# Moving the row scaling and the folds within the first 66 slots of a fused top-k attention and expert kernel

## The chip, the cores and the metric

The kernel runs on one core of one Trainium2 chip. The metric is the device time of one execution, in microseconds (us); lower is better. The engines are TensorE (PE, with its weight loads PEld), VectorE (DVE), ScalarE (ACT), GpSimd (POOL) and the queue of SyncE (SP), which here only issues DMAs. Each engine works through its own list of instructions in order, and waits on semaphores for what others produce.

## The reference: what is computed

Attention in which each query keeps only its 32 largest scores, and then a layer of eight experts of which each token takes one:

```python
batch, n_heads, seq, head_dim = (8, 8, 576, 64)
scores = scale * np.matmul(q, k.transpose(0, 1, 3, 2))
kth = np.partition(scores, -top_k, axis=-1)[..., -top_k:-top_k + 1]
scores = np.where(scores >= kth, scores, -1000000000.0)
attn = np.exp(scores - np.max(scores, axis=-1, keepdims=True))
attn = attn / (np.sum(attn, axis=-1, keepdims=True) + 1e-09)
x = np.matmul(attn, v)             # then (B, H, S, D) -> (B*S, H*D) = (4608, 512)
logits = x @ w_gate                # 8 experts; the largest logit takes the token
h = np.maximum(x_sorted[lo:hi] @ w1[e], 0.0)     # 512 -> 1024
y_sorted[lo:hi] = h @ w2[e]                      # 1024 -> 512
out = gate_w[:, None] * y
```

## The kernel before

**Slots.** The attention is cut into tiles of 128 queries by 576 keys, and two tiles make one slot. The main loop (L1217) makes 144 passes, i = 0 to 143: 18 slots for each of the 8 batches. A batch has four units of two heads; two units share nine slots (four slots of the first, one of both units' last 64 queries, four of the second). Below, "slot 12" is the pass with i = 12.

**One slot on VectorE.** `fold` (L307) takes the maximum `h` (L313) and the minimum `l` (L314) of the two halves of the next slot's scores. `fold_on` (L317) folds `h` once more: its maximum goes to `few` (L320), its minimum to `hl`. That minimum is made either on DVE (L328) or, when `aside_too` holds, on POOL by two integer operations, sum (L325) and difference (L326). `lists` (L345, L349) takes the eight largest of `l` and of the halves of `hl`. `search` (L351) then finds the 32 largest in four rounds, r = 0 to 3: MAX8 (L372) on both tiles and, in all but the last, MATCH_REPLACE (L382), which takes the eight found away. With `soon`, `fold_on` for the next slot comes after round r = 1; without it, before the last round's MAX8. From r = 2 on, `tick` (L332) puts one small step from the list `aside` behind each instruction: divisors, choice of experts, ranks, and the table of blocks.

**The other engines in a slot.** In round 0, POOL makes the bias `nbias` (L378). After the search, ACT makes `low` (L393) and `w` (L409); POOL subtracts, `w = s - w` (L418, one instruction per tile), and stores `doubt` (L399); ACT copies the scores of a later slot out of PSUM (L304), copies the transposed weights of the slot before (L444 or L442, L461), and makes the exponentials (L426) of this slot's `w`. PE makes scores (L297), transposes (L437), output products (L474, L485), and pieces of the expert blocks (L948, L965). The order on PE, ACT and DVE is the order of the code; on POOL most instructions are kept in it by `in_turn` (L250), while its indirect DMAs (L590 scatters rows of x, L857 stores rows of the result) are placed by the scheduler.

**The end of a unit.** `ending` (L1080) is a generator that a slot with tile 3 starts. It yields names of places, and the loop calls `at_place(name)` (L1176) where it may go on: "relu" copies outputs out of PSUM (L476, L492) and makes divisors (L496 to L501), "rows" (L1109) scales on POOL: `logits` (L511, then L513 and L514, or L516 in a batch's first unit), and `rows` (L525, 128x640). In the kernel before, "relu" and "rows" both stand behind `less` and `doubts` (L1242, L1243), and "relu" ahead of the scores of L304. For the last unit of a batch the generator goes on to the choice, the ranks, the scatter and the table that says which expert blocks can be loaded.

**Crowded slots.** `k.crowded` is set by the scaling of rows (L520), by stores (L1036) and by scatters (L1072). The next slot then doesn't search with `soon`. The integer fold is used only where 0 < i < `QUIET` (48) and the slot isn't crowded.

Of the kernel before, what the change touches and what calls it, by code (L numbers as in the profile page):

```python
# [44 lines left out]
def kernel(  # L45
# [48 lines left out]
    B, U, P, _ = qk.shape  # L94
# [37 lines left out]
    k = SimpleNamespace()  # L132

    def open_pools(st, exact):
        for name, bufs in (
            ("load", 2), ("att", 2), ("xp", 1 if exact else 2), ("small", 2),
            ("wp", 1 if exact else 2), ("mlp", 2),
        ):
            setattr(k, name, st.enter_context(tc.tile_pool(name=name, bufs=bufs)))
        for name, bufs in (("ps_s", 2), ("ps_t", 2), ("ps_m", 2)):  # L140
            pool = tc.tile_pool(name=name, bufs=bufs, space=bass.MemoryType.PSUM)
            setattr(k, name, st.enter_context(pool))
        k.exact = exact
        k.apart = k.between = k.crowded = False

    def load_unit(b, u, parts=False):
        n = SimpleNamespace(b=b, u=u)
# [102 lines left out]
    def in_turn(put):  # L250

        if not k.exact:
            tc.keep_in_program_order(put)
        return put
# [62 lines left out]
    def fold_on(f, aside_too=False):  # L317

        f.few = k.att.tile([P, 2, LW], F32, name="few", bufs=3)
        nc.vector.tensor_tensor(f.few[:, :, 0:QF], f.h[:, :, 0:QF], f.h[:, :, QF:HF], op=ALU.max)  # L320
        hl = k.att.tile([P, 2, QF], I32, name="hl", bufs=1)
        f.hl, f.aside = hl[:, :, :].bitcast(F32), aside_too
        if aside_too:
            one, other, more = (a.bitcast(I32) for a in (f.h[:, :, 0:QF], f.h[:, :, QF:HF], f.few[:, :, 0:QF]))
            in_turn(nc.gpsimd.tensor_tensor(hl, one, other, op=ALU.add))  # L325
            in_turn(nc.gpsimd.tensor_tensor(hl, hl, more, op=ALU.subtract))  # L326
        else:
            nc.vector.tensor_tensor(f.hl, f.h[:, :, 0:QF], f.h[:, :, QF:HF], op=ALU.min)  # L328

    aside = []  # L330

    def tick():  # L332

        while aside:
            if next(aside[0], "end") != "end":
                return
            aside.pop(0)
# [10 lines left out]
            for j, away in enumerate((f.l[:, m, :], f.hl[:, m, 0:QF // 2], f.hl[:, m, QF // 2:QF])):  # L348
                nc.vector.max(out=f.few[:, m, QF + 8 * j:QF + 8 * j + 8], in_=away)  # L349

    def search(tiles, s, f, then=lambda: None, soon=False, behind=lambda: None):  # L351

        m_all = range(2)
        tops = k.small.tile([P, 2, TOP_K], F32, name="tops", bufs=4)
        if k.exact:
            src = [s[:, m, :, :].rearrange("p j k -> p (j k)") for m in m_all]
            width = S
        else:
            src = [f.few[:, m, 0:QF] for m in m_all]
            width = LW  # L360
            if not f.aside:
                lists(f)
        behind()
        scr = k.att.tile([P, 2, width], F32, name="scr", bufs=1)
        nbias = k.small.tile([P, 2], F32, name="nbias", bufs=3)
        R = TOP_K // 8

        for r in range(R):
            if r == R - 1 and not soon:
                then()  # L370
            for m in m_all:
                nc.vector.max(out=tops[:, m, r * 8:(r + 1) * 8], in_=src[m])  # L372
                if r > 1:
                    tick()
            if r == 1 and soon:
                then()
            if r == 0:
                in_turn(nc.gpsimd.tensor_scalar_mul(nbias, tops[:, :, 0], -scale))  # L378
            if r < R - 1:
                for m in m_all:  # L380
                    first = r == 0 and not k.exact
                    nc.vector.match_replace(  # L382
                        out=src[m] if first else scr[:, m, :], in_to_replace=tops[:, m, r * 8:(r + 1) * 8],
                        in_values=src[m], imm_value=NEG,
                    )
                    if r > 1:
                        tick()
                    src[m] = f.few[:, m, :] if first else scr[:, m, :]
                if first and f.aside:
                    lists(f)  # L390
        thr = tops[:, :, TOP_K - 1]
        low = k.small.tile([P, 2], F32, name="low", bufs=3)
        nc.scalar.activation(low, thr, AF.Copy, scale=STEEP)  # L393

        def doubts():
            n, i = tiles[0]
            at = n.b * U + n.u
            over = doubt[:, at:at + 2, 2 * NC, :] if tails(tiles) else doubt[:, at, 2 * i:2 * i + 2, :]
            k.last_pool = in_turn(nc.gpsimd.tensor_tensor(  # L399
                over, f.few[:, :, QF + 7:LW:8], _inner(thr, NL), op=ALU.subtract  # L400
            )).ins

        return low, nbias, doubts
# [581 lines left out]
    FIRST = 13  # L985
    ARRIVED = 13
    AHEAD = 3
    QUIET = 48
    ON_CHIP = 3
    KEEP = 3 * PIECES  # L990
    BETWEEN = 2
# [1 line left out]
    with fast:  # L993
# [86 lines left out]
        def ending(b, u):  # L1080
# [68 lines left out]
            if new:  # L1149
                if b == B - 1:  # L1150
                    slot_i = slot_last
                    steps = end_table(slot_i, slot_long, new, half, full)
                else:
                    slot_i = k.small.tile([1, 2, NSLOT], I32, name="slot_i")
                    steps = table(slot_i, new, False)
                aside.append(steps)
                yield "weights"
                yield "pool"
                yield "weights"
                yield "pool"  # L1160
                through(steps)
                coming.extend((slot_i[0:1, 0, j:j + 1], slot_i[0:1, 1, j:j + 1]) for j in range(new))
            if b == B - 1:
# [10 lines left out]
        late = []  # L1174
# [25 lines left out]
        def loop():  # L1200
# [16 lines left out]
            for i, (b, g) in enumerate(work):  # L1217
                tiles = tiles_of(i)
                u, tile = g[0]
                if tile == 0 and u % 2 == 0:  # L1220
                    open_unit(tiles[0][0])
                if tails(tiles):
                    open_unit(tiles[1][0])

                then, quiet = lambda: None, 0 < i < QUIET and not k.crowded
                behind = lambda: None
                if i + 1 < len(work):
                    def behind():
                        f_of[i + 1] = fold(s_of[i + 1])

                    then = lambda: fold_on(f_of[i + 1], quiet)
                    if i:
                        behind()
                        behind = lambda: None
                low, nbias, doubts = search(tiles, s_of[i], f_of.pop(i), then, quiet, behind)
                k.crowded = False
                at_place("small")
                w_of[i] = depths(s_of[i], low)
                less(s_of.pop(i), w_of[i])
                doubts()  # L1240
                at_place("pool")
                at_place("relu")  # L1242
                at_place("rows")  # L1243
                put_stores()
                scatter(1)
                at = i % per_batch
                if at == FIRST and b:
                    rate = level(b) * PIECES / (U * NT)
                credit += rate * len(g)
                room = left  # L1250
                if b == B - 1 and at >= ARRIVED:
                    room -= KEEP
                    credit = room / (len(work) - i)
                share = {0: 0.5, 1: 1.2, 2: 1.6, 3: 0.5, 2 * NC: 1.4}[tile]
                now = max(0, min(int(credit * share + 0.5), room))
                credit -= now
                clock = i
                if i + AHEAD < len(work):
                    s_of[i + AHEAD], steps = scores(got_of.pop(i + AHEAD))
                    for step in steps:  # L1260
                        step()
                evacuate()
                at_place("turn")
                turns = turning(i - 1) if i else iter(())
                next(turns, None)
                part = min(BETWEEN, now - now // 2)
                rest = pieces(part)
                next(turns, None)
                rest = pieces(now - now // 2 - part + rest)
                weights(tiles, w_of[i], nbias)  # L1270
                next(turns, None)
                evacuate()
                if i + AHEAD + 1 < len(work):
                    multiply(i + AHEAD + 1)
                if tile == NC - 1:
                    end = ending(b, u)
                    late.append([end, next(end)])
                at_place("products")
                at_place("weights")
                credit = min(credit + pieces(now // 2 + rest), 6 * rate)  # L1280
# [152 lines left out]
```

## Time and profile before

| what | value |
|---|---|
| median of 3 runs | 1304.83 us (1302.8 to 1308.25) |
| the profiled execution | 1303.64 us, its span 1302.0 us |
| granted TensorE clock, mean | 0.967 |
| L418 on POOL, w = s - w | x288, 407.0 us busy, 1434 ns each; idle before it 342.6, waiting for ACT's L409 |
| L372 on DVE, MAX8 on 168 elements | x576 from `scr`, 165.9 us, 316 ns each |
| L313 and L314 on DVE, 128x576 | x143 each, 108.9 and 109.3 us, 761 and 764 ns |
| L320 on DVE, 128x288 | x144, 79.2 us, 550 ns |
| L328 on DVE, 128x288 | x114, 52.3 us, 459 ns |
| L325 and L326 on POOL, the integer fold | x30 each, 793 and 834 ns |
| L525 on POOL, 128x640 | x32, 42.0 us, 1312 ns |
| L476 on ACT, outputs out of PSUM | x64, 25.1 us; idle before it 32.4, waiting for PE's L474 |

A line of the profile names the source line, the engine, the operation, what is written and read, shape and count; behind the bar stand busy time, mean duration of one, and the idle time just before. An instruction that an engine has begun but that can't go on counts as busy, so a duration above the usual one of its kind is also something to look for. The page's second part shows busy tenths in 40 slices of the span. In the timeline each row is start, duration, engine, line, operation; in square brackets is the idle time before it and what ended it. Rows of the same kind that follow each other are merged (x2).

### The profile page before, as it was taken

To read this page: it belongs to the slowest core of one execution; us is meant where nothing else is said; L and a number is where in the kernel's file an instruction comes from. 1 tells how busy PE (TensorE), PEld (TensorE's weight loads), DVE (VectorE), ACT (ScalarE), POOL (GpSimd) and SP (SyncE) were. 2 spreads that over 40 slices of the span, in tenths; PEclk is the share of its full clock that TensorE was granted. 3 is DMA by queue.
4 is the path that set the end of the run, shared out by engine and by line. 5 is a ranking of instruction groups with operands and counts; after the bars stand their busy time and mean duration, and the time that the engine had idled before them with its cause. 6 is when DMAs were issued, how large, how long until landed. Compare 5 with 4: busy or idle time off the path is not lost. (4 is left out here: it accounts for less than half of the span.)

```text
span 1302.0 us, 24603 instructions
## 1 busy us (share of the span) xinstructions
PE 1193.9 (92%) x7654; PEld 836.4 (64%) x7654; DVE 1065.2 (82%) x4589; ACT 931.6 (72%) x2136; POOL 716.9 (55%) x867
## 2 busy tenths in 40 slices
PE   6777776899989999999999999999999999999998
PEld 3444443665666556666666666666666677789975
DVE  8999999999999999999999999999999954000000
ACT  4888877898888888888788888798888861112121
POOL 4777776777755575658555755576557643000010
PEclk9888888899999999999999999999999999999999
DMA  5000112741374148533945465447555458986682
GB/s 151 30 30 30 30 38 94 277 166 38 123 267 160 39 139 306 183 111 122 331 135 213 142 240 179 171 137 250 175 176 188 162 206 261 354 311 230 213 291 87
DMA packets 98797, 220.95 MB, mean 170 GB/s; under 512 B 5341, under 2 KB 26333, under 8 KB 98656
## 3 DMA queue, kind: packets, MB, share of 16 engines
q1 hardware_dynamic: 91424, 199.00, 44.4%
q0 software_dynamic: 6416, 19.97, 4.2%
q8 instruction: 62, 1.02, 0.3%
q14 instruction: 79, 0.65, 0.2%
q10 hardware_dynamic: 816, 0.31, 0.1%
HBM read 195.88 MB, written 24.17 MB: 169 GB/s over the span
## 5 line engine op out<-in xcount | busy, mean ns | idle before, releaser
L418 POOL TENSOR_TENSOR w<-s,w 128x576 f32<-128x576 f32 x288 | 407.0, 1434 | 342.6 <-ACT w L409 342.5
L948 PE MATMUL ph<-xTs,w 128*128 128x128 f32 x2112 | 259.7, 277 | 4.5 <-ACT xTs L839 3.0
L948 PEld LDWEIGHTS ph<-xTs,w 128*128 128x128 f32 x2112 | 248.0, 192 | 23.0 <-issue 17.6
L965 PE MATMUL py<-w,hT 128*128 128x512 f32 x528 | 248.2, 599 | 3.3 <-ACT hT L953 3.2
L426 ACT ACTIVATE w<-w,nbias 128x576 f32<-128x576 f32 x288 | 224.1, 793 | 2.8 <-POOL w L418 2.1
L409 ACT ACTIVATE w<-s,low 128x576 f32<-128x576 f32 x288 | 207.6, 768 | 4.7
L297 PE MATMUL sc<-qkb 64*128 64x288 f32 (+1 forms) x1280 | 201.8, 465 | 8.3 <-DMA qkb<-in_qk_dram 4.2
L437 PE MATMUL wTm<-turn,w 128*128 128x128 f32 x1152 | 169.9, 288 | 24.3 <-ACT oT L476 10.9
L437 PEld LDWEIGHTS wTm<-turn,w 128*128 128x128 f32 x1152 | 133.3, 146 | 81.2 <-issue 34.3
L304 ACT COPY s<-sc 128x576 f32<-128x576 f32 x288 | 168.7, 639 | 9.9 <-PE sc L297 9.9
L372 DVE MAX8 tops<-scr 128x8 f32<-128x168 f32 x576 | 165.9, 316 | 0.0
L444 ACT COPY wT<-wTm 128x512 f32<-128x512 f32 x256 | 139.0, 604 | 24.8 <-PE wTm L437 24.7
L372 DVE MAX8 tops<-few 128x8 f32<-128x144 f32 (+1 forms) x576 | 151.9, 303 | 0.0
L474 PE MATMUL po<-wT,vb 128*64 128x288 f32 x1024 | 151.6, 443 | 0.0
L297 PEld LDWEIGHTS sc<-qkb 64*128 64x128 f32 (+1 forms) x1280 | 107.1, 189 | 69.2 <-issue 31.4
L965 PEld LDWEIGHTS py<-w,hT 128*128 128x128 f32 x528 | 91.9, 191 | 88.0 <-issue 82.6
L857 POOL DMA_INDIRECT out_dram<-y,xg x37 | 38.9, 1052 | 172.7 <-ACT y L974 87.4
L349 DVE MAX8 few<-l 128x8 f32<-128x288 f32 x288 | 127.7, 443 | 0.0
L474 PEld LDWEIGHTS po<-wT,vb 128*64 128x64 f32 x1024 | 73.2, 148 | 74.5 <-issue 24.9
L313 DVE TENSOR_TENSOR h<-s 128x576 f32<-128x576 f32 (+1 forms) x145 | 109.8, 757 | 4.5 <-ACT s L304 4.1
L314 DVE TENSOR_TENSOR l<-s 128x576 f32<-128x576 f32 (+1 forms) x145 | 110.2, 760 | 0.0
L349 DVE MAX8 few<-hl 128x8 f32<-128x72 f32 x576 | 100.1, 213 | 0.0
(190 smaller groups left out, 1607.6 us busy)
## 6 DMA issues: line engine op xcount, KB each, us to landing
w<-in_moe_w_dram SPq DMA_DIRECT2D x74, 2048.0 KB, 9.1
qkb<-in_qk_dram SPq DMA_DIRECT2D x31, 608.0 KB, 4.0
vb<-in_v_dram SPq DMA_DIRECT2D x32, 320.0 KB, 3.2
xg<-x_rows SPq DMA_DIRECT2D x37, 257.0 KB, 9.6
x_rows<-blank SPq DMA_DIRECT2D x13, 257.0 KB, 8.9
x_rows<-blank POOLq DMA_DIRECT2D x4, 257.0 KB, 8.3
x_rows<-x,posi POOLq DMA_INDIRECT x40, 3.3
out_dram<-y,xg POOLq DMA_INDIRECT x37, 4.0
```

The costliest lines, as they stand in the source:

```text
L297: nc.tensor.matmul(ps[rows, j, 0:HF], n.q[d, cols], n.k[d, keys], start=True, stop=True)
L304: lambda m=m, ps=ps: nc.scalar.copy(s[:, m, :, :], ps[:, :, 0:HF]) for m, ps in enumerate(got)
L349: nc.vector.max(out=f.few[:, m, QF + 8 * j:QF + 8 * j + 8], in_=away)
L372: nc.vector.max(out=tops[:, m, r * 8:(r + 1) * 8], in_=src[m])
L409: nc.scalar.activation(w[:, m, :], s[:, m, :, :].rearrange("p j k -> p (j k)"), AF.Relu, scale=-STEEP, bias=low[:, m:m + 1],)
L418: k.last_pool = in_turn(nc.gpsimd.tensor_tensor(w[:, m, :], s[:, m, :, :].rearrange("p j k -> p (j k)"), w[:, m, :], op=ALU.subtract)).ins
L426: nc.scalar.activation(w[:, m, :], w[:, m, :], AF.Exp, scale=scale, bias=nbias[:, m:m + 1], accum_out=n.z[:, c:c + 1])
L437: nc.tensor.transpose(pm[:, c * P:(c + 1) * P], w[:, m, first:first + P], ident)
L444: nc.scalar.copy(wT[:, :, m, q], pm4)
L474: nc.tensor.matmul(po[r, 0:HF], n.v[:, c, r], rhs, start=(c == 0), stop=(c == KC - 1))
L948: nc.tensor.matmul(ph[:, f, :], n.w1[:, 0, dt, fc * P:(fc + 1) * P], n.xT[:, dt, :], start=(dt == 0), stop=(dt == DT - 1),)
L965: nc.tensor.matmul(py, hT[:, f, :], n.w2[:, 0, f, :], start=(f == 0), stop=(f == FT - 1))
```

## The change

- A slot is now called heavy (`k.heavy`) when 0 < i < `QUIET` and the rows of a unit are due in it. In a heavy slot the rows are scaled inside `search`, right behind `nbias` of round 0 (`beside`), and no longer at the end of the slot before; the next slot's folds (L320, L328) come behind round r = 1, with the minimum on DVE; and `tick` puts in no small steps. A heavy slot also hands on whether it was itself crowded.
- `QUIET` goes from 48 to 66. So slots 48 to 65 that aren't crowded use the integer fold on POOL.
- For 0 < i < `QUIET`, "relu" (outputs out of PSUM, divisors) comes behind the copy of the scores (L304) and no longer ahead of it.
- The table of blocks gets three rounds of places and not two, in all batches but the last.

```diff
-        k.apart = k.between = k.crowded = False
+        k.apart = k.between = k.crowded = k.heavy = False
...
     def tick():
 
-        while aside:
+        while aside and not k.heavy:
             if next(aside[0], "end") != "end":
...
-    def search(tiles, s, f, then=lambda: None, soon=False, behind=lambda: None):
+    def search(tiles, s, f, then=lambda: None, soon=False, behind=lambda: None, beside=lambda: None):
...
             if r == 0:
                 in_turn(nc.gpsimd.tensor_scalar_mul(nbias, tops[:, :, 0], -scale))
+                beside()
...
-    QUIET = 48
+    QUIET = 66
...
                 aside.append(steps)
-                yield "weights"
-                yield "pool"
-                yield "weights"
-                yield "pool"
+                for _ in range(3 if b < B - 1 else 2):
+                    yield "weights"
+                    yield "pool"
                 through(steps)
...
-                then, quiet = lambda: None, 0 < i < QUIET and not k.crowded
-                behind = lambda: None
+                loose = 0 < i < QUIET
+                k.heavy = loose and "rows" in [place for _, place in late]
+                soon = loose and (k.heavy or not k.crowded)
+                then = behind = beside = lambda: None
                 if i + 1 < len(work):
                     def behind():
                         f_of[i + 1] = fold(s_of[i + 1])
 
-                    then = lambda: fold_on(f_of[i + 1], quiet)
+                    then = lambda: fold_on(f_of[i + 1], soon and not k.heavy)
                     if i:
                         behind()
                         behind = lambda: None
-                low, nbias, doubts = search(tiles, s_of[i], f_of.pop(i), then, quiet, behind)
-                k.crowded = False
+                if k.heavy:
+                    beside = lambda: at_place("rows")
+                held = k.heavy and k.crowded
+                low, nbias, doubts = search(tiles, s_of[i], f_of.pop(i), then, soon, behind, beside)
+                k.crowded, k.heavy = held, False
                 at_place("small")
                 w_of[i] = depths(s_of[i], low)
                 less(s_of.pop(i), w_of[i])
                 doubts()
                 at_place("pool")
-                at_place("relu")
-                at_place("rows")
+                if not loose:
+                    at_place("relu")
+                    at_place("rows")
                 put_stores()
                 scatter(1)
...
                     for step in steps:
                         step()
+                if loose:
+                    at_place("relu")
                 evacuate()
                 at_place("turn")
```

## The prediction

> **What bounds the kernel now.** I read the page's busy tenths first, then the answer by windows, then the timeline of single slots. A slot is one pass of the main loop, i = 0 to 143; its length is the time from the end of the previous slot's eighth MAX8 of L372 to the end of its own.
>
> ```profile
> PE 1193.9 (92%) x7654; PEld 836.4 (64%) x7654; DVE 1065.2 (82%) x4589; ACT 931.6 (72%) x2136; POOL 716.9 (55%) x867
> ...
> PE   6777776899989999999999999999999999999998
> ...
> DVE  8999999999999999999999999999999954000000
> ```
>
> PE has the largest total, but VectorE is full until slice 33 and stops there. By windows:
>
> ```profile
> 187.00:240.00 53.00, 36.77 (x203) 21.85 (x202) 53.00 (x217) 39.83 (x93) 34.70 (x41) 0.77 0.45 160
> 240.00:360.00 120.00, 111.91 (x759) 76.25 (x757) 119.45 (x515) 104.98 (x246) 90.85 (x109) 0.99 0.37 130
> 360.00:488.00 128.00, 117.52 (x786) 78.59 (x785) 128.00 (x565) 110.16 (x258) 78.99 (x96) 0.99 0.42 147
> 640.00:1057.00 417.00, 410.92 (x2787) 284.92 (x2786) 416.64 (x1760) 355.49 (x823) 256.69 (x304) 1.00 0.53 184
> 1057.00:1302.00 245.00, 237.22 (x1427) 194.49 (x1425) 15.86 (x90) 48.50 (x92) 31.50 (x38) 1.00 0.72 246
> ```
>
> The third number is the stretch, then busy PE, PEld, DVE, ACT, POOL. Up to 1057 us DVE has no gap worth naming: the attention loop lasts as long as DVE's instructions. Then 245 us of PE work remain. What DVE saves before slot 66 (it ends at 487.9) shortens the run one for one as long as PE, idle for 8.1 and 10.5 us of the second and third stretch, can follow.
>
> DVE's "busy" hides waits, and they are what this change is about. An undisturbed slot with the integer fold on POOL lasts 6.55 us (slots 9, 13, 16), one with L328 on DVE 6.92 (slots 49, 54, 56). Slot 12 lasts 7.49:
>
> ```profile
> 96.56 1.26 POOL L525 TENSOR_TENSOR x<-xl,rz 128x640 f32<-128x640 f32 x1
> ...
> 97.12 1.01 DVE L320 TENSOR_TENSOR few<-h 128x288 f32<-128x288 f32 x1
> ...
> 102.89 0.54 POOL L399 TENSOR_TENSOR doubt<-few,tops 128x6 f32<-128x6 f32 x1
> 102.94 0.43 DVE L320 TENSOR_TENSOR few<-h 128x288 f32<-128x288 f32 x1
> ```
>
> L320 takes 0.43 alone and 1.01 while POOL multiplies rows: it waited till about 97.70, just ahead of the shown end of L525 (97.82). In slot 13 the small L399 waits for L320 instead. The worst case:
>
> ```profile
> 196.50 0.26 POOL L516 TENSOR_TENSOR lg<-xl 128x40 f32<-128x40 f32 x1
> 196.61 4.16 DVE L659 TENSOR_TENSOR past<-past,step_all 1x24 f32<-1x24 f32 x1
> 196.73 1.25 POOL L525 TENSOR_TENSOR x<-xl,rz 128x640 f32<-128x640 f32 x1
> 197.95 2.75 POOL L418 TENSOR_TENSOR w<-s,w 128x576 f32<-128x576 f32 x2
> ```
>
> A step on 24 elements of one partition stands for 4.16 us behind rows and two subtractions in a row; slot 27 lasts 11.48. A third habit:
>
> ```profile
> 420.36 1.05 POOL L511 TENSOR_TENSOR xl<-xl,rz 128x80 f32<-128x80 f32 x1
> 420.41 0.45 DVE L320 TENSOR_TENSOR few<-h 128x288 f32<-128x288 f32 x1
> 420.78 0.46 DVE L328 TENSOR_TENSOR hl<-h 128x288 f32<-128x288 f32 x1
> ```
>
> When DVE's pair L320, L328 runs back to back, POOL (0.33 us of work) waits for both.
>
> **What the Trainium skill says.** "SBUF — State Buffer", section "Who interferes with whom": a DVE instruction with two SBUF inputs contends with a GpSimd instruction that reads SBUF, the lock is exclusive, and issue order decides who blocks. The lines above agree (1.01 against 0.43), and MAX8 and MATCH_REPLACE keep 0.32 us beside L418. "Perfetto Trace Analysis", section "GPSIMD Engine Instruction", calls POOL's spans unreliable and wants start-to-start spacing; so I take starts where I can (L511 to L525 is 0.98 us in slot 12).
>
> **The change part by part.** In the built order PE's sequence is unchanged, and nothing on any engine differs after slot 67.
>
> *Slots with rows.* They are 8, 12, 17, 21, 26, 30, 35, 39, 44, 48, 53, 57, 62. Rows now follow L378 of that slot, so they stand before its L418, and L320, L328 come after round two, at +3.96 us. Undisturbed, L418 of the slot before runs from +1.12 to +3.96 (slot 13), so the pair takes +3.96 to +4.78; L399 waits for it and ends at +4.85, L378 at +5.03; L511 to L525 takes 0.98, L525 1.26: it ends at +7.24 and lets DVE in at +7.12. The next L313 comes at 6.92 - 0.08 = +6.84 and waits 0.28. Sum 7.20. So slot 12 gains 7.49 - 7.20 = 0.29, 21 0.28, 30 0.29, 48 0.29, 53 0.36. Slot 17, where ACT is 0.27 late, gets about 0.1 more: 7.69 - 7.30 = 0.39. Slot 8 has the short form without L513 (L511 to L525 0.63): L525 ends at +6.89, no stall, 7.34 - 6.92 = 0.42. Together 2.32.
>
> *Slots 26 to 28.* Slot 26 becomes heavy and takes no small steps, so L659 moves to slot 27, where rows no longer stand in front of L418. Slot 26: 6.92 plus 0.4 behind a late L418. The indirect DMA (1.03 us) stands before L378, so rows end late and hold the next L313 by about 0.95. Slot 27: 6.92 + 0.95 + 0.4 for the steps; slot 28: 6.92 + 0.4. Sum 22.9 against 7.90 + 11.48 + 7.06 = 26.44: gain 3.5. If L418 stays as late as now (+2.74), it is 1.0 less.
>
> *Slots 44 and 62* have the same shape: their table steps move one slot on. Slots 43 to 46 last 30.58 now; I take 29.6 (heavy slot 6.92, the next 6.92 + 0.45 + 0.3 for steps behind a late L418): 1.0. Slots 62 to 64: 22.55 to 21.6, 0.95. *Slots 39 and 57* have an indirect DMA ahead of the rows; L525 slips into the next slot behind L313 and L314, as it does now: gain 0.
>
> *Scores ahead of outputs.* ACT waits in order for po:
>
> ```profile
> 185.70 0.65 PE L474 MATMUL po<-wTt,vb 128*64 128x288 f32 x4
> ...
> 186.40 0.40 ACT L476 COPY oT<-po 128x288 f32<-128x288 f32 x1 [2.90 <-PE po L474]
> 186.70 1.19 ACT L304 COPY s<-sc 128x576 f32<-128x576 f32 x2
> ```
>
> The scores of L304 were there; copied inside the idle 2.90 us they take 1.05 off ACT's lateness. Copies add no work; the price is PE waiting for a po bank up to 1.05 longer, hidden while ACT would idle anyway, and uncovered where po is ready first. It pays only where L418 stops being late: slots 11 and 20 lose 0.23 each to it, I take half, 0.23; slots 33 to 35 (7.02 + 7.43 + 8.44 = 22.89) I put at 22.0, gain 0.9.
>
> *Integer fold up to slot 66.* L328 leaves DVE in slots 49, 50, 52, 54, 55, 56, 59, 60 and returns in 40: 114 to 107. Seven new slots at 6.92 - 6.55 = 0.37 are 2.6, slot 52 with its late L418 0.27: 2.87. But where ACT is late, L320 at +3.96 stands behind L418: of the ten integer slots between 31 and 42, slots 33, 34 and 41 lost 0.47, 0.88, 0.65. With shorter slots ACT has less room (110.16 of 128 us). I take half: 1.4. Slot 40 is in slots 39 to 41, which I leave at 21.3.
>
> *Third table round, SP order.* Two loads (qkb, vb) pass the first batch's row and weight loads, which now come one slot later. Nothing: xg (222.92) waits for the last scatter (219.53), not for the table. If that cover went, PE's first expert work (243.21) would slip by up to one slot, 7 us, of which PE's idle would return most.
>
> Sum: 2.32 + 3.5 + 1.0 + 0.95 + 0.23 + 0.9 + 1.4 = 10.3 us. Span 1302.0 - 10.3 = 1291.7; plus the 1.64 around it 1293.3. The median stands 1.2 above that execution (1304.83 against 1303.64): 1294.5.
>
> **Bounds.** If every excess over 6.55 or 6.92 in slots 8 to 62 goes (0.45 more for five small steps, slot 24's 7.00 - 6.55, left in), that is 15.8, and the fold brings its 2.6: 18.4, 1286.4. Below nothing: see the third rival.
>
> **Rivals.** *All stalls go* (1287): needs ACT on time everywhere; slots 13 to 16 show that it happens, slots 33 to 35 speak against.
>
> *The gain is taken up by ACT and PE* (1301.6): from slot 48 on many slots show PE busy throughout (51, 52, 56), and shorter slots only make L418 late, so that new integer slots, 33 to 35 and 43 to 64 bring nothing. Left are slots 8 to 30 (0.42 + 0.29 + 0.39 + 0.28 + 0.23 + 3.5 + 0.29 = 5.4), and of these I keep six tenths: 3.2. Against it: 10.5 us of PE idle in that stretch.
>
> *Slower* (1314): the pair at +3.96 meets the second L418 wherever ACT is late, waiting its 1.41 us, and rows then stand whole (1.26) in front of the next L313. A heavy slot then costs 6.92 + 1.41 + 1.26 = 9.59, against 7.68, the mean of the 13 now: 1.9 more. In ten of them that is 19, against 9.5 for all else (3.5 + 1.0 + 0.95 + 0.23 + 0.9 + 2.87): 9.5 us slower. It decides once the 13 lose over 9.5 / 13 = 0.73 us on average; slots 26, 44 and 62 are near it, 12, 21, 30 and 48 are not, since their L418 is on time.
>
> **How the numbers follow.** Forecast 1294.5 with 0.64 (its own range 1290 to 1299), all stalls 0.06, taken up 0.19, slower 0.11. Range 1287 to 1304: it holds the first two and most of the third. 0.5% is 6.5 us, about what a measurement of this kernel can tell from no change (the three times spread over 5.5). The forecast and the first rival give faster 0.70; taken up is same, 0.19; slower 0.11.
>
> **What would show it.** Right: L328 x107, L325 x37; no L659 over 1 us; L320's mean down from 550 ns; slot 12 near 7.2, slots 26 to 28 near 23; the last MAX8 near 1047 us and about 245 us after it. Wrong: L320 over 1 us in heavy slots at +3.96, L313 over 1.2, DVE gaps waiting for L304, or a tail longer than 245.

## The result, and the profile after

The changed kernel takes 1295.31 us (median of 12 runs, 1291.45 to 1300.21), the kernel before 1302.85 (12 runs, 1300.63 to 1308.25): ratio 0.9941, 95% interval 0.9923 to 0.9959. The profiled execution took 1294.12 us, its span 1292.5.

Two times are used throughout: medians of several runs, and slot lengths read from one profiled execution of each kernel. From L379 on, the changed kernel's line numbers are one higher: L419 is the old L418.

The page's first part, and its tenths for PE and DVE:

```profile
PE 1185.8 (92%) x7654; PEld 835.0 (65%) x7654; DVE 1057.5 (82%) x4582; ACT 934.1 (72%) x2136; POOL 730.1 (56%) x881
...
PE   6776776999899999999999999999999999999998
...
DVE  8999999999999999999999999999999954000000
```

The picture is the same, DVE full up to slice 33. Its busy time fell by 7.7 us, and DVE's last MAX8 of slot 143 now ends at 1049.34 us where it ended at 1057.37: 8.0 us. The windows, cut at the shifted places:

```profile
236.00:352.00 116.00, 107.46 (x729) 73.49 (x729) 116.00 (x506) 100.89 (x236) 84.53 (x102) 0.99 0.36 121
352.00:480.00 128.00, 117.86 (x788) 79.75 (x786) 128.00 (x555) 111.28 (x259) 90.84 (x108) 0.97 0.43 149
631.00:1049.00 418.00, 411.92 (x2796) 285.75 (x2795) 417.34 (x1763) 356.33 (x826) 257.61 (x305) 1.00 0.53 184
1049.00:1292.50 243.50, 237.12 (x1427) 194.40 (x1425) 15.83 (x90) 48.45 (x92) 31.47 (x38) 1.00 0.72 248
```

DVE (third busy time) still has no gap up to 1049; after it, 243.2 us of tail instead of 244.7. The 1.5 us of tail are one wait of PE for weights by DMA that this execution did not have; profiles of five variants below have it again (0.9 to 2.0 us), so I don't count it for the change.

Slot 12 and the start of slot 13, in the timeline:

```profile
94.90 0.90 POOL L400 TENSOR_TENSOR doubt<-few,tops 128x6 f32<-128x6 f32 x1
94.93 0.44 DVE L320 TENSOR_TENSOR few<-h 128x288 f32<-128x288 f32 x1
95.29 0.45 DVE L328 TENSOR_TENSOR hl<-h 128x288 f32<-128x288 f32 x1
...
96.91 1.26 POOL L526 TENSOR_TENSOR x<-xl,rz 128x640 f32<-128x640 f32 x1
97.82 0.97 DVE L313 TENSOR_TENSOR h<-s 128x576 f32<-128x576 f32 x1
```

L320 lasts 0.44 (1.01 before). The rows (L526, the old L525) meet the next L313 now, which lasts 0.97 instead of 0.74. Slots 26 to 28:

```profile
193.62 0.73 DVE L313 TENSOR_TENSOR h<-s 128x576 f32<-128x576 f32 x1
193.65 2.49 POOL L526 TENSOR_TENSOR x<-xl,rz 128x640 f32<-128x640 f32 x1
194.28 0.74 DVE L314 TENSOR_TENSOR l<-s 128x576 f32<-128x576 f32 x1
196.10 2.77 POOL L419 TENSOR_TENSOR w<-s,w 128x576 f32<-128x576 f32 x2
...
201.19 0.15 DVE L660 TENSOR_TENSOR past<-past,step_all 1x24 f32<-1x24 f32 x1
```

The step that stood 4.16 us (L659, now L660) takes 0.15. Here the rows wait for both L313 and L314: they are shown as 2.49 long, though they need 1.26.

The gain came in the early slots, not in the late ones. This table gives the sums of slot lengths (us) from the timelines, for the two kernels, for a second profile of the changed one, and for three variants that are described below:

| slots | before | changed | changed, second profile | outputs first (e1) | outputs first from 36 (e5, second profile) | e5 with scatters behind rows (e9) |
|---|---|---|---|---|---|---|
| 1–25 | 170.51 | 168.36 | 169.77 | 170.95 | 169.55 | 169.69 |
| 26–29 | 33.36 | 29.04 | 30.85 | 31.18 | 30.86 | 28.94 |
| 30–38 | 63.22 | 60.81 | 61.89 | 62.26 | 61.87 | 60.83 |
| 39–42 | 28.29 | 28.60 | 28.61 | 28.00 | 28.00 | 28.00 |
| 43–47 | 37.50 | 37.50 | 37.40 | 37.51 | 36.45 | 36.44 |
| 48–60 | 92.39 | 90.47 | 90.66 | 89.03 | 89.00 | 89.04 |
| 61–65 | 36.85 | 38.75 | 37.43 | 37.54 | 37.62 | 37.47 |
| 66–68 | 21.34 | 21.70 | 21.34 | 21.33 | 21.33 | 21.33 |
| 69–143 | 555.65 | 555.63 | 555.62 | 555.71 | 555.65 | 555.69 |
| all | 1039.11 | 1030.86 | 1033.57 | 1033.51 | 1030.33 | 1027.43 |

Slots 1 to 38 gain 8.9 us (4.6 in the second profile), slots 39 to 68 lose 0.65 (gain 0.93 in the second). A first hint at where the late gain went is the answer by waits (engine, tile and line waited at, what ended it; us in total over the whole run, times, longest). First the kernel before, then the changed one:

```profile
ACT oT L476 <- PE po L474: 32.3, 43, 2.9
ACT wT L444 <- PE wTm L437: 24.7, 20, 3.2
PE wTm L437 <- ACT oT L476: 10.9, 8, 5.6
```

```profile
ACT wT L445 <- PE wTm L438: 35.9, 49, 3.2
PE wTm L438 <- ACT oT L477: 29.5, 22, 3.1
...
ACT oT L477 <- PE po L475: 18.7, 28, 2.5
```

ACT waits 13.6 us less for po, as the new order of copies meant. But PE's transposes wait 18.6 us more for the outputs' copies, now behind the scores, and ACT then waits 11.2 us more for those transposes. Another wait of PE, at L453 (now L454) for ACT's copies of the transposed weights, falls by 27.0 us, so the waits alone don't say which way the balance goes: they cost time only where DVE waits at their end. The experiments decide it.

### The profile page after: what moved, and what is told of

It is laid out like the page before. It is cut to its first block, busy times and chain, and to the rows that moved or that the text cites. A ratio compares the mean times of both kernels' runs of the same rounds, so it can differ in the third digit from the quotient of the medians.

```text
span 1292.5 us, 24591 instructions
## 1 busy us (share of the span) xinstructions
PE 1185.8 (92%) x7654; PEld 835.0 (65%) x7654; DVE 1057.5 (82%) x4582; ACT 934.1 (72%) x2136; POOL 730.1 (56%) x881
## 3 DMA queue, kind: packets, MB, share of 16 engines
q8 instruction: 62, 1.02, 0.3%
## 5 line engine op out<-in xcount | busy, mean ns | idle before, releaser
L419 POOL TENSOR_TENSOR w<-s,w 128x576 f32<-128x576 f32 x288 | 407.5, 1436 | 320.6 <-ACT w L410 320.5
L304 ACT COPY s<-sc 128x576 f32<-128x576 f32 x288 | 167.9, 634 | 11.7 <-PE sc L297 11.6
L475 PE MATMUL po<-wT,vb 128*64 128x288 f32 x1024 | 141.6, 420 | 0.0
L313 DVE TENSOR_TENSOR h<-s 128x576 f32<-128x576 f32 (+1 forms) x145 | 110.4, 761 | 4.2 <-ACT s L304 4.2
L475 PEld LDWEIGHTS po<-wT,vb 128*64 128x64 f32 x1024 | 69.3, 140 | 67.1 <-issue 14.7
L314 DVE TENSOR_TENSOR l<-s 128x576 f32<-128x576 f32 (+1 forms) x145 | 110.8, 764 | 0.0
```

What stands on the lines that cost most here:

```text
L304: lambda m=m, ps=ps: nc.scalar.copy(s[:, m, :, :], ps[:, :, 0:HF]) for m, ps in enumerate(got)
L419: k.last_pool = in_turn(nc.gpsimd.tensor_tensor(w[:, m, :], s[:, m, :, :].rearrange("p j k -> p (j k)"), w[:, m, :], op=ALU.subtract)).ins
L475: nc.tensor.matmul(po[r, 0:HF], n.v[:, c, r], rhs, start=(c == 0), stop=(c == KC - 1))
```

## The experiments

In what follows "the port" is what a two-input instruction of DVE and an instruction of POOL were seen to wait for each other at, as L320 and the rows do in slot 12.

**Outputs ahead of scores again (e1_relu_first).** In the changed kernel:

```diff
                 at_place("pool")
+                at_place("relu")
                 if not loose:
-                    at_place("relu")
                     at_place("rows")
...
-                if loose:
-                    at_place("relu")
```

> The changed kernel, but outputs are copied out of PSUM ahead of the scores again in every slot. Port theory (DVE's length is its own work plus waits for POOL's port, and ACT's order only moves L418): slots 1 to 38 lose about 3 us (11 and 20 0.23 each, 26 to 29 about 1, 33 to 36 about 1.5), because ACT idles ahead of L476 again; slots 39 to 65 win about 5, because PE gets its po bank back sooner and the 9.27 us slot 61 falls below 8. Net about 2 us faster than the changed kernel: 1293. Rival (the order on ACT carries the gain): back to 1301 or above, slots 39 to 65 not better.

Measured: 1294.21 us (1293.62 to 1300.02), ratio 0.9927 (0.9913 to 0.994), not told apart from the changed kernel. Inside it two effects cancel: in the profiles, slots 1 to 38 take 6.2 us longer than the changed kernel's (1.9 longer than in its second profile), slots 39 to 65 take 3.2 less (2.0). Of the 3.2, 1.2 are slot 61, which lasts 8.06 here, but 8.03 in the second profile of the changed kernel too, so it is not the order that made it 9.27. Scores ahead of outputs pays early and costs late.

**Integer fold only to slot 48 (e2_quiet48).**

```diff
-    QUIET = 66
+    QUIET = 48
```

> The changed kernel with QUIET at 48: from slot 48 on everything is as in the kernel before, heavy slots too. Port theory: slots 48 to 60 lose the 1.9 us that they had won (90.47 to 92.4), slots 61 to 65 win back the 1.9 that they had lost (38.75 to 36.9); time unchanged, 1295 within 1. Rival (the seven L328 that leave DVE are the gain, 7 x 0.459): 3.2 us slower, 1298.5.

Measured: 1297.03 us (1292.9 to 1298.88), ratio 0.9952 (0.9938 to 0.9966). By time alone that is not told apart from the changed kernel; it lies between the 1295 expected and the rival's 1298.5. `QUIET` also ends the other parts of the change. Slots 48 to 60 go back to 91.74 and slots 61 to 65 to 36.88: what slots 48 to 60 gain by it is 1.3 us (1.1 against the second profile), not the rival's 3.2, and slots 61 to 65 give 1.9 back (0.55).

**No heavy slots (e3_no_heavy).** Rows are scaled at the end of the slot, behind the outputs:

```diff
-                k.heavy = loose and "rows" in [place for _, place in late]
+                k.heavy = False
...
                 if loose:
                     at_place("relu")
+                    at_place("rows")
```

> The changed kernel without heavy slots: rows are scaled at the end of the slot, behind the output copies, the next slot is crowded and folds before the last round, small steps everywhere. Port theory: slots 8, 12, 17, 21, 30, 35, 48, 53 are back near 7.4 to 7.6, 0.4 to 0.6 more each, some 3 us; slots 26 to 29 lose 2 to 4 more, as steps stand behind rows and L418 again; 1299 to 1302. Rival (QUIET and the order on ACT are the gain): 1295 to 1297.

Measured: 1298.43 us (1296.81 to 1299.84), ratio 0.9963 (0.9949 to 0.9977). The medians can't tell it from the changed kernel (0.9941 and, run again, 0.9956); the slots can. Slots 12, 21, 30 and 48 are back at 7.47 to 7.49, where heavy slots last 6.92. Slots 26 to 29 take 29.94: the 4.16 us of L659 are gone without heavy slots too. In slot 26 the rows stand 1.0 us earlier there (+6.93 us from the slot's start, +7.95 before), a step ahead of L660 waits for them (1.21 us), and L660 itself comes behind them and takes 0.15.

**The kernel before without small steps behind rows (e4_before_no_steps).** Only this and the third round are taken over from the change; it holds up to slot 65 (rows of slot 65 included):

```diff
-        while aside:
+        while aside and not k.heavy:
...
-                yield "weights"
-                yield "pool"
-                yield "weights"
-                yield "pool"
+                for _ in range(3 if b < B - 1 else 2):
+                    yield "weights"
+                    yield "pool"
...
-        k.crowded = True
+        k.crowded = k.rowed = True
...
+                k.heavy, k.rowed = 0 < i < QUIET + 18 and k.rowed, False
```

> The kernel before, with one part of the change alone: no small steps in the slots whose rows were put on POOL just before (8 to 62), and a third table round. Port theory: the 4.16 us L659 goes, slots 26 to 29 from 33.36 to about 29, slots 43 to 47 and 61 to 65 win 0 to 1 each, all others as before: 4 to 6 us faster than before, 1298. Rival (the long L659 is only how the profile shows an idle stretch, and DVE waits for something else there): slots 26 to 29 stay above 32, time as before, 1303.

Measured: 1302.1 us, ratio 0.9984 (0.9973 to 0.9995): about 2 us faster. Slots 26 to 29 fall from 33.36 to 29.61 as expected; slots 1 to 25, 43 to 47 and 61 to 65 together take 3.9 us longer in the profile. A miss: 4 to 6 us were expected. Of the 3.9, 1.4 are slots 6 and 11, where L320 stands behind a late L418 and not behind a step. The rest is made by the edit. Slot 44 falls from 8.54 to 7.02, but DVE, without its steps, then comes to the next folds while POOL is still at the rows, and slot 45 takes 9.62 where it took 7.00:

```profile
324.84 1.25 POOL L525 TENSOR_TENSOR x<-xl,rz 128x640 f32<-128x640 f32 x1
324.97 1.75 DVE L313 TENSOR_TENSOR h<-s 128x576 f32<-128x576 f32 x1
...
326.64 1.96 DVE L314 TENSOR_TENSOR l<-s 128x576 f32<-128x576 f32 x1
```

Slot 63 does the same (9.63). Taking away one stall of 4.16 us is not 4 us of the kernel when it moves DVE into another meeting.

**Rows scaled twice (e6_rows_twice).** In the kernel before, to measure the port by itself:

```diff
         in_turn(nc.gpsimd.tensor_tensor(xu, xl, _inner(rzb, D), op=ALU.mult))
+        in_turn(nc.gpsimd.tensor_tensor(xu, xl, _inner(rzb, D), op=ALU.mult))
```

> The kernel before, with the scaling of rows (128x640) issued twice in a row; the result is the same. Theory (a DVE instruction with two inputs waits for POOL's run of instructions to end): in each of the 13 slots that put rows ahead of L320 or L313, that instruction waits up to 1.26 us more: 10 to 16 us slower in slots 7 to 62, about 1313 to 1319, and L659 in slot 27 stands near 5.4 us. Rival (DVE waits for one instruction of POOL only, and POOL has idle time to take the second one): under 5 us slower.

Measured: 1315.18 us (1314.25 to 1317.25), ratio 1.0095 (1.0075 to 1.0116): 11.4 us slower, 11.3 in the sum of slots. Slots 7 to 62, for which 10 to 16 were expected, make up 8.7 of it; the rest comes after, since the rows are doubled in all 32 places. Slot 12 of it in the timeline:

```profile
97.44 1.26 POOL L525 TENSOR_TENSOR x<-xl,rz 128x640 f32<-128x640 f32 x1
98.00 1.01 DVE L320 TENSOR_TENSOR few<-h 128x288 f32<-128x288 f32 x1
98.78 1.35 POOL L526 TENSOR_TENSOR x<-xl,rz 128x640 f32<-128x640 f32 x1
98.94 1.51 DVE L328 TENSOR_TENSOR hl<-h 128x288 f32<-128x288 f32 x1
```

L320 waits for the first scaling and L328 (0.45 alone) for the second: slot 12 goes from 7.49 to 8.54, 1.05 us for one POOL instruction of 1.26. In such a meeting (slots 8, 12, 17, 21, 30, 48 and 53 lose 1.04 to 1.29 each) POOL's time is paid nearly in full; in slots 35, 44 and 62, each with the slot behind it, the second scaling costs 0.0 to 0.2. The expected 5.4 us of L659 (L660 here) did not come: it took 1.40, waited for the first scaling alone and got in ahead of the second, and slot 27 is even shorter than before (8.72). So a run of POOL's instructions does not always keep DVE out to its end. One difference between the two runs is that the second scaling writes the same tile as the first and begins 0.08 us after it has ended (203.00 to 203.08), while L418, in slot 27 of the kernel before, followed the rows without a gap. Whether the gap let DVE in is not shown; in slot 12 L328 began 0.16 us behind the second scaling and waited for it.

**Two rounds for the table (e7_two_rounds).** In the changed kernel:

```diff
-                for _ in range(3 if b < B - 1 else 2):
+                for _ in range(2):
```

> The changed kernel with two rounds of places for the table of blocks instead of three, as before the change. The prediction put the third round at nothing: 1295 within 1.5, slots 26 to 30 within 0.3 us of the changed kernel's. Rival (the table's small steps get behind the last searches in time only with the third round, and are otherwise run in one piece, DVE stopping the loop): a slot of each batch longer by 1 to 3 us, 1298 or more.

Measured: 1300.77 us (21 runs, 1298.22 to 1303.97), ratio 0.9979 (0.9971 to 0.9986); beside it the changed kernel took 1297.04. The rival was right. Start of slot 45:

```profile
325.19 1.26 POOL L526 TENSOR_TENSOR x<-xl,rz 128x640 f32<-128x640 f32 x1
325.25 0.20 ACT L394 ACTIVATE low<-tops 128x2 f32<-128x2 f32 x1 [0.17 <-DVE tops L372]
325.36 1.11 DVE L664 SCALAR_TENSOR_TENSOR slot_f<-slot_f,done,slots_less 1x3 f32<-1x3 f32 x1
326.41 2.78 POOL L419 TENSOR_TENSOR w<-s,w 128x576 f32<-128x576 f32 x2
326.50 1.34 DVE L669 TENSOR_TENSOR slot_i<-slot_f,upto_max 1x6 int32<-1x6 f32 x1
327.77 0.15 DVE L674 TENSOR_SCALAR upto_max<-upto_max 1x9 f32<-1x9 f32 x1
327.96 1.25 DVE L676 TENSOR_TENSOR left<-upto_max 1x8 f32<-1x8 f32 x1
```

A heavy slot takes no small steps, so two rounds are over before the table is done, and `through` runs the rest in one piece, at the place where POOL has rows and two subtractions in a row: three steps on 3 to 8 elements stand for 3.7 us, L313 starts 4.2 us late. Slot 45 lasts 11.09 (8.45 in the changed kernel), slot 63 11.29 (8.47).

**The changed kernel again (after_again).**

> The changed kernel once more, unaltered, beside the others on the same chip. If slot 45 (8.45 us) and the stall of PE in the tail (0 to 2 us) are chances of an execution and not of the program, this run shows other values for them with all of slots 1 to 42 within 0.1 us of the first profile; the time within 1291 to 1300. If they belong to the program, slot 45 is 8.45 again.

Measured: 1297.04 us (1296.59 to 1299.13), ratio 0.9956 (0.9941 to 0.9971). Slot 45 is 8.44 again, but slots 17, 20, 27 and 35 are 7.66, 6.99, 9.32 and 7.88, where they were 6.99, 6.55, 7.57 and 6.92: my "within 0.1 us" was wrong, and for slot 45 neither answer fits: 8.44 here, but 7.41 in e2_quiet48, whose program is the same up to slot 47. Slot 27 shows what differs:

```profile
194.65 1.26 POOL L526 TENSOR_TENSOR x<-xl,rz 128x640 f32<-128x640 f32 x1
194.95 1.57 DVE L313 TENSOR_TENSOR h<-s 128x576 f32<-128x576 f32 x1
196.16 3.50 POOL L419 TENSOR_TENSOR w<-s,w 128x576 f32<-128x576 f32 x2 [0.26 <-ACT w L410]
196.44 1.95 DVE L314 TENSOR_TENSOR l<-s 128x576 f32<-128x576 f32 x1
```

In the first profile L313 began 0.03 us ahead of the rows, and both folds went first. Here the rows began 0.30 ahead of L313: it waits for them, and L314 then waits for the first subtraction. The price of that order is 9.32 - 7.57 = 1.75 us.

**Outputs first from slot 36 on (e5_relu_mix, e5_again).** Each order of copies where e1_relu_first showed it to pay:

```diff
-                if not loose:
+                if not loose or i >= 36:
                     at_place("relu")
+                if not loose:
                     at_place("rows")
...
-                if loose:
+                if loose and i < 36:
                     at_place("relu")
```

> The changed kernel, but from slot 36 on outputs are copied ahead of the scores again, as before the change; up to slot 35 they stay behind. Theory (behind the scores saves time early, where POOL's subtraction is late for want of scores, and costs time late, where the transposes wait for the outputs' copies): slots 1 to 38 as in the changed kernel (258.2 us), slots 39 to 65 near 192 instead of 195.3, so 2 to 3 us less: 1292 to 1293 where the changed kernel reads 1295. Rival (the late losses come from PE being full, whatever the order of the copies): slots 39 to 65 stay at 195 and the time at 1295.

Measured: 1292.92 us (1291.94 to 1293.35), ratio 0.992 (0.9903 to 0.9936); all five runs lie below all six of the changed kernel beside it. In its first profile slots 39 to 65 take 191.89 us, against 195.32 and 194.10; slots 1 to 38 are like those of the second profile.

> e5_relu_mix once more, beside e8_store_later. If the order of the copies decides slots 39 to 65, they take 191.9 us again and the time is 1292.9 within 1. If the lengths of slots 17, 20, 27 and 35 (7.57, 6.93, 9.33 and 7.87 in its first profile; 6.99, 6.55, 7.57 and 6.92 in the first profile of the changed kernel) are chances of an execution, some of them differ now, and the sum of slots 11 to 36 lies between 179.0 and 183.0 us.

Measured: 1293.95 us (1292.26 to 1294.96), ratio 0.9931 (0.9918 to 0.9945). Slots 39 to 65 take 191.07, so the order of copies decides them, but 1.04 of that is slot 45, 7.40 this time. Slots 17, 20, 27 and 35 repeat themselves to 0.03 us, against what was expected; the sum of slots 11 to 36 is 183.05, just outside what was said. Slot 42 shows the effect itself: 7.59 with scores first, where L320 waits for a late L419 (1.02 us), 7.00 with outputs first (0.44). First the changed kernel, then e5_again:

```profile
299.54 2.77 POOL L419 TENSOR_TENSOR w<-s,w 128x576 f32<-128x576 f32 x2 [2.17 <-ACT w L410]
301.61 1.02 DVE L320 TENSOR_TENSOR few<-h 128x288 f32<-128x288 f32 x1
```

```profile
302.88 2.77 POOL L419 TENSOR_TENSOR w<-s,w 128x576 f32<-128x576 f32 x2 [1.54 <-ACT w L410]
305.58 0.44 DVE L320 TENSOR_TENSOR few<-h 128x288 f32<-128x288 f32 x1
```

**A store's DMA behind the rows (e8_store_later).** In e5_relu_mix:

```diff
-                put_stores()
+                if not (loose and [1 for _, place in late if place in ("relu", "rows")]):
+                    put_stores()
```

> The kernel of e5_relu_mix, in which the row store's indirect DMA (L858) of slots 44 and 62 comes behind that slot's rows and the next slot's subtractions, not ahead of the bias; nothing else moves on POOL, nothing on PE or DVE. Theory (slots 45 and 63 last 8.45 because the DMA's 1.03 us pushes the rows onto the next slot's L313 and L314, with which they contend for the port): rows end near +7.2 us of slot 44 as in slot 48, L313 of slot 45 waits 0.25, slot 45 lasts near 7.3 instead of 8.44, slot 63 as well: 2.2 us in sum, 1290.7 where e5_relu_mix reads 1292.9. Rival (slots 45 and 63 are long for ACT or PE, or the moved DMA makes as much delay in slot 45): slots 43 to 47 within 0.3 of 37.44 and the time at 1292.9.

Measured: 1295.92 us (1294.14 to 1296.29), ratio 0.9944 (0.993 to 0.9957), against 1293.95 of e5_again beside it. The profile has 1.3 us of that in slots 1 to 25 (mostly slot 8, 7.60 against 6.92), which the edit doesn't touch. The expectation named the wrong slots. What moved was in slots 39 and 57; in 44 and 62 the DMA ahead of the rows is a scatter, L591, and it stayed. In 39 and 57 the rows came in time (+5.94 us), yet slots 40 and 58 last 7.70 and 7.69 instead of 7.53: L313 waits 0.23 there, and nothing is gained, since slot 40's rows had already stood behind L313 and L314 (+0.75) and cost DVE only 0.1. Slot 45 was 8.45 and slot 63 7.41, neither touched by the edit.

**The scatter's DMA behind the rows (e9_scatter_behind).** The right instruction, in e5_relu_mix:

```diff
-                    beside = lambda: at_place("rows")
+                    def beside():
+                        at_place("rows")
+                        if kept_back:
+                            k.last_pool = k.last_row
+                            scatter(1)
...
-                scatter(1)
+                kept_back = i in (25, 43, 61)
+                if not kept_back:
+                    scatter(1)
```

> The kernel of e5_relu_mix, in which in the heavy slots 26, 44 and 62 the scatter's indirect DMA (L591, 1.03 us) comes behind the rows and no longer ahead of the bias; nothing else moves on POOL, nothing on PE, DVE or ACT. Theory (that DMA pushes the rows onto the border of the next slot, where the rows and L313, L314 contend for the port and DVE loses 1.0 to 1.8 us whenever POOL wins): rows start at +5.94 as in slot 48, L313 of the next slot lasts 0.97 and L314 0.75. Slots 26 to 29 then take 28.9 instead of 30.8, slot 45 near 7.4 whatever the execution, slot 63 near 7.4: 3 to 4 us less than e5_relu_mix's 1292.9 to 1294.0, so about 1290. Rival (as in e8_store_later, where rows in time brought nothing for slots 40 and 58, the five small steps and a late L419 set these slots): the three groups stay at 30.8, 36.4 to 37.4 and 37.5, and the time at 1293.

Measured: 1290.19 us (1289.76 to 1291.63), ratio 0.9893 (0.9876 to 0.9909): faster than every other version here; the nearest, e5_relu_mix, has 0.9903 to 0.9936. In the slots it is 2.9 to 3.4 us less than e5_relu_mix's two profiles, where 3 to 4 were expected. First the border of slots 44 and 45 in the changed kernel, then here:

```profile
320.22 0.73 DVE L313 TENSOR_TENSOR h<-s 128x576 f32<-128x576 f32 x1
320.25 1.82 POOL L526 TENSOR_TENSOR x<-xl,rz 128x640 f32<-128x640 f32 x1
...
320.88 1.81 DVE L314 TENSOR_TENSOR l<-s 128x576 f32<-128x576 f32 x1
322.03 3.30 POOL L419 TENSOR_TENSOR w<-s,w 128x576 f32<-128x576 f32 x2
```

```profile
318.71 1.26 POOL L526 TENSOR_TENSOR x<-xl,rz 128x640 f32<-128x640 f32 x1
...
319.96 0.73 DVE L313 TENSOR_TENSOR h<-s 128x576 f32<-128x576 f32 x1
...
320.13 2.14 POOL L591 DMA_INDIRECT x_rows<-x,posi  x1 [0.15 <-issue]
320.62 0.74 DVE L314 TENSOR_TENSOR l<-s 128x576 f32<-128x576 f32 x1
```

The rows end with the slot, even earlier than expected, and L313 and L314 last 0.73 and 0.74. Slots 26 to 29 take 28.94 (expected 28.9), slot 45 7.39 and slot 63 7.41. The DMA lasts 2.14 us beside the two folds (1.03 in its old place) and still costs nothing: the second L419 of slot 45 ends where it ended in the changed kernel, at +5.05 us, and L320 is not due before +6.02. Slot 61 was 9.05 in this profile (8.05 in e5_again), which took 1 us of the gain back. There is one profile of this kernel; in slots 27, 45 and 63 of it the rows are at their end when L313 begins, so the meeting itself is gone.

## Why the prediction was right

The forecast was 1294.5 us, faster, and 1295.31 came out. Point by point:

- *What bounds it.* Right. In every profile the time is DVE's last MAX8 and a tail of 243 to 247 us, and slots 69 to 143 take the same 555.6 us in both kernels. The tail was 243.2 us, not 245; the last MAX8 at 1049.3, not 1047.
- *Heavy slots.* Right. L320's mean fell from 550 to 531 ns, with 107 instructions of L328 and 37 of L325. Slots 12 and 13 together gain 0.34 (said: 0.29 for slot 12; the wait of L313 counts in slot 13). Slots 8, 12, 17, 21 and 30, each with its successor (slot 8 alone), gain 1.98 us in the first profile and 1.30 in the second, where 1.67 was said. e6_rows_twice shows the mechanism, e3_no_heavy which slots it shortens. Two of the named signs of being wrong did come in the second profile: L320 lasts 1.17 at +3.95 in heavy slot 17, and L313 1.57 in slot 27.
- *Slots 26 to 28.* Right in kind: no L660 over 0.17 us. The sum was said to be 22.9 and was 21.97 in one profile and 23.80 in the other. The 0.95 us that I gave to rows behind the indirect DMA is really either about 0 or about 1.75, depending on who takes the port first (a third outcome, 8.37 for slot 27 in e1_relu_first, has L313 first and L314 behind the rows).
- *Slots 44 and 62: the step that failed.* I wrote that they have "the same shape" and took 0.3 for the slot after, so 1.0 and 0.95 us of gain. Slots 45 and 63 lasted 8.44 to 8.47 in both profiles of the changed kernel, and slots 43 to 47 gained 0.0 to 0.1. The DMA stands ahead of the rows there too, and I had priced it in slot 26 but not here. e9_scatter_behind moves it, and 1.0 us comes back in each of the two slots.
- *Scores ahead of outputs.* The mechanism and its price were named, the balance was not. Slots 11, 20 and 33 to 35 gained 2.8 in the first profile and 1.2 in the second, against the 1.1 that I took. The price ("uncovered where po is ready first") I put at nothing; e1_relu_first and e5_relu_mix show it at 2.0 to 2.3 us in slots 39 to 65, with slot 61 left out.
- *Integer fold.* Half of its 2.87 was right for slots 48 to 60: with the heavy slots they gained 1.9 and 1.7, where 2.05 was said. e5_relu_mix explains the half: with outputs first the same slots gain 3.4, nearly the whole 3.5. But slot 61, which I had left alone, went from 7.38 to 8.03 and 9.27. It is 7.40 where `QUIET` is 48 and 8.0 or more in every version with 66, in both orders of copies, so it belongs to the new integer slots: ACT is late there, and small steps wait behind L419.
- *Third round.* Nothing, I wrote, and looked only at the loads on SP. Its real work is to make room for the small steps that heavy slots put off; without it slots 45 and 63 lose 5.5 us in the profile. The sum did not suffer, since it never contained that loss.
- *The sum.* Said 10.3 us; the slots give 8.25 and 5.54, the medians 7.5 and 6.7. By stages it fits less well, and the sum owes something to luck: slots 1 to 38 were given 6.3 us and gained 8.9 and 4.6, slots 39 to 68 were given 4.0 and lost 0.65 and gained 0.93. The level was nearer than the difference because the before I started from, 1304.83, was the median of three runs and stood 2 us above the median of twelve.

Of the rivals, "all stalls go" is out; "taken up by ACT and PE" describes slots 39 to 68 well in size, but not the early ones, and not by its reason: e5_relu_mix and e9_scatter_behind win there without taking work from PE or ACT; "slower" is out: no heavy slot came near 9.59.

Not settled: why ACT is late in slots 17 and 20 of one profile and not of the other, why slots 6 and 8 vary between profiles of kernels that are the same up to there (6.62 to 7.16 and 6.92 to 7.73), and why slot 61 is 8.04 in some profiles and 9.05 or 9.27 in two.

## What to carry to other kernels

When GpSimd work is moved, ask for each place what two-input VectorE instruction it will meet there, and what else (a DMA issue of 1 us) is queued ahead of it: the same move gained 1.0 us more in slots 45 and 63 once that DMA stood behind it. The best order of two copies on one engine can differ between stages of one loop, so test it by stage and not for the whole. And where a step is held back, count the room that it needs later.

## What the runs showed of the hardware

The Trainium skill, "SBUF — State Buffer", section "Who interferes with whom", says that issue order decides who blocks. At a first meeting the runs agree: in slot 27 L313 went first where it began 0.03 us ahead of the rows, and waited where it began 0.30 behind them. For what comes next they show more than that rule: at the start of slot 45 the rows are issued 0.03 to 0.05 us behind L313 in all seven profiles in which slot 44 is heavy, the scatter stands ahead of the rows and the table has three rounds. L314 comes some 0.6 us after the rows, and yet at the end of L313 the port went to L314 in two of these (e2_quiet48, e5_again; slot 45 7.4) and to the waiting rows in five (8.45). The chip does not decide it: e1_relu_first and e2_quiet48 ran on one chip, e5_again and e8_store_later on another, and each pair has both lengths. A program with such a meeting has two times for it, and one profile shows only one of them.

The loser can also wait for more than one instruction: L313 and L314 back to back held the rows for 1.23 us (2.49 - 1.26), while the rows and a subtraction held L313 and L314 in turn for 0.83 and 1.21 us (1.57 - 0.74 and 1.95 - 0.74).
